# A drain on GpSimd's queue behind an expert's last gather, and row scatters without waits for one another

## The chip, the cores and the metric

One core of one Trainium2 chip runs the kernel in one launch. The metric is the device time of that launch in microseconds, as the median of several runs. The engines are named as in the profile: PE (TensorE), DVE (VectorE), ACT (ScalarE), POOL (GpSimd), SP (SyncE); PEld is TensorE's weight loading. A name with a q behind it (POOLq) means the instructions of that engine's queue: waits, branches, drains.

## What is computed

Attention with two kinds of masks, a dense feed-forward layer, and a layer of eight experts of which each token visits one, on 2304 tokens of width 512. The last of the three is what the change is in:

```python
def _moe2_ref(x, w_skip, w_gate, w1, w2):
    do_compute = x @ w_skip > 0
    out = x.copy()
    xc = x[do_compute]
    logits = xc @ w_gate
    e_idx = np.argmax(logits, axis=1)
    probs = softmax(logits)
    gate_w = probs[np.arange(len(xc)), e_idx]
    for e in range(E):
        mask = e_idx == e
        h = np.maximum(xc[mask] @ w1[e], 0.0)
        y[mask] = gate_w[mask, None] * (h @ w2[e])
    out[do_compute] = xc + y
```

## The kernel before

Attention and the dense layer run first, in an order that a planner in the kernel writes out. The routing is done block by block beside them: `route_list` (L822, 18 DMAs issued by GpSimd) writes each token's number and weight into the list of its expert, `lst`. The layer's result goes into `out` and `x2d` in DRAM, so a token that visits no expert is done.

`experts()` then goes through the lists in tiles of 128 tokens, four tiles to a group. `gather` (L888) reads four tiles of rows out of `x2d` by four indirect DMAs of GpSimd; `turn` transposes them; `up` (L920) is the first matrix of the expert, `down` (L933) the second, one output tile of 128 rows after the other. For each such tile VectorE scales the result and adds the gathered row (`row`, L937), and GpSimd scatters the tile into `out` (L938), an indirect DMA that writes each row where the list says. The places come from the list alone; entries behind a list's end are outside the bounds and write nothing.

Which expert comes first is guessed before the routing ends, and its weights and first four tiles are fetched early. The rest of a list is worked off by `groups`: full groups of four tiles under nested conditions, and then `rest` with the one to three tiles left over. The group's gather for what comes next is issued inside the group that comes before it. So `rest` gathers four tiles for the next expert (L1093) between the first two and the last six of its eight steps of `up`, and then its own `down` scatters its tiles.

With these inputs one expert has the list: one early group of four tiles (its scatters stand under L1057 and L1076 in the program's conditions), three full groups, and `rest` with two tiles (the branch of L1106). The loop over further experts (L1117, L1118) is not entered. Behind the loop the program ends (L1376): each engine drains, SyncE waits for the semaphores' last values, and the engines meet in an exchange of semaphores that GpSimd leads.

The framework sets the waits. GpSimd's DMAs count their landings on eight semaphores, the lanes DMASW0 to DMASW7, used in turn. Two writes into the same DRAM tensor are put in order: a scatter into `out` waits until the scatter before it has landed. Where a branch is not taken, an instruction of GpSimd (INC_SWDGE_SEM, "ISA" in the order) raises the lanes by what the branch would have added: all eight at the end of L1076, one in the branch of L1106, all eight at L1117. VectorE writes rows into three buffers in turn, and waits for the scatter that last read the buffer.

Of the kernel before, what the change touches and what calls it, by code (L numbers as in the profile page):

```python
# [189 lines left out]
def kernel(  # L190
# [18 lines left out]
    PE, V, A, G, SY = nc.tensor, nc.vector, nc.scalar, nc.gpsimd, nc.sync  # L209
# [542 lines left out]
    def route_a(blk):  # L752
        d = rt[blk]
        lg = d["lg"]
        l8 = lg[:, :, 0:8]
        mx = sp.tile([128, 12], F32, name="mx")
        e8 = sp.tile([128, 3, 8], F32, name="e8")
        d.update(mx=mx, e8=e8)
        V.tensor_reduce(mx[:, 0:3], l8, axis=AX.X, op=ALU.max)
        V.tensor_tensor(e8[:], l8, bc(mx[:, 0:3]), op=ALU.is_equal)  # L760
        V.tensor_tensor(l8, l8, bc(mx[:, 0:3]), op=ALU.subtract)
# [4 lines left out]
    def route_exp(blk):  # L766
        d = rt[blk]
        d["x8"] = sp.tile([128, 3, 8], F32, name="x8")
        A.activation(d["x8"][:], d["lg"][:, :, 0:8], AF.Exp)
# [21 lines left out]
    def route_c(blk):  # L791
        d = rt[blk]
        mx = d["mx"]
        d["pay"] = pay = sp.tile([128, 3, 2], I32, name="pay")
        V.tensor_reduce(mx[:, 9:12], d["x8"][:], axis=AX.X, op=ALU.add)
        V.tensor_scalar_add(mx[:, 9:12], mx[:, 9:12], 1e-9)
        V.reciprocal(pay[:, :, 1].bitcast(F32), mx[:, 9:12])
        V.tensor_copy(pay[:, :, 0], toks[:, 3 * blk:3 * blk + 3])
# [31 lines left out]
    def reg(t, c, hi, on=None):  # L830
        kw = {} if on is None else {"engines": on}
        return nc.values_load(t[0:1, c], min_val=0, max_val=hi, skip_runtime_bounds_check_because=WHY, **kw)

    def tally(cn):
        PE.matmul(cn[:, 0:8], one, cum[0][:, 3, :], start=True, stop=True)
# [48 lines left out]
    def gather(gi, n=NT):  # L884
        gx = sp.tile([128, 4], I32, name="gx")
        V.tensor_copy(gx[:], gi)
        for t in range(4):
            G.indirect_dma_start(  # L888
                K["R"][t], None, x2d[0:n, :], bass.IndirectOffsetOnAxis(ap=gx[:, t:t + 1], axis=0),
                bounds_check=n - 1, oob_is_err=False,  # L890
            )
# [22 lines left out]
    def up(N, f0=0, f1=NFE):  # L914
        for f in range(f0, f1):
            p = ph.tile([128, 512], F32, name="h")
            n = 0
            for w, x in ((0, K["Xh"]), (1, K["Xh"]), (0, K["Xl"])):
                for k in range(4):
                    PE.matmul(p[:, 0:N], W[f][:, w, k * 128:(k + 1) * 128], x[:, k, 0:N], start=n == 0, stop=n == 11)  # L920
                    n += 1
            h = K["h"][f]
            A.activation(h[:, 0, 0:N], p[:, 0:N], AF.Relu)  # L923
            V.scalar_tensor_tensor(h[:, 1, 0:N], p[:, 0:N], 0.0, h[:, 0, 0:N].bitcast(F32), op0=ALU.max, op1=ALU.subtract)  # L924

    def down(nt, ids, rows, t0=0):
        for t in range(t0, nt):
            c = slice(t * 128, (t + 1) * 128)
            y = px.tile([128, DM], F32, name=f"x2p{K['ny'] % 3}")
            n = 0  # L930
            for f in range(NFE):
                for g, w in ((0, 0), (1, 0), (0, 1)):
                    PE.matmul(y[:], K["h"][f][:, g, c], W[NFE + f][:, w, :], start=n == 0, stop=n == 3 * NFE - 1)  # L933
                    n += 1
            yo = rp.tile([128, DM], F32, name="row")
            K["ny"] += 1
            V.scalar_tensor_tensor(yo[:], y[:], ids[:, t, 1:2].bitcast(F32), rows[t], op0=ALU.mult, op1=ALU.add)  # L937
            G.indirect_dma_start(  # L938
                out, bass.IndirectOffsetOnAxis(ap=ids[:, t, 0:1], axis=0),
                yo[:], None, bounds_check=NT - 1, oob_is_err=False,  # L940
            )

# [73 lines left out]
    def keep_rows():  # L1018
        for t in range(4):
            A.copy(K["E"][:, t, :], K["R"][t])  # L1020

    def experts():
        K["h"] = [wp.tile([128, 2, 512], F32R, name=f"wo{8 + f}") for f in range(NFE)]
        K["E"] = wp.tile([128, 4, DM], F32, name="xb2")
        E = [K["E"][:, t, :] for t in range(4)]
        npre = reg(pre, slice(3, 4), NT)

        def fill(n):
            lo, hi = FILL[n], FILL[n + 1]
            if hi > lo:  # L1030
                with tc.If(npre >= 512):
                    up(512, lo, hi)

        last_x2(fill)
        route_a(NBLK - 1)
        route_exp(NBLK - 1)
        route_b(NBLK - 1)
        route_c(NBLK - 1)
        keep_rows()
        fill(3)  # L1040
        rk, cn = (pm.tile([128, 512], F32, name=n_) for n_ in ("sx0", "sx1"))
        route_rank(NBLK - 1, rk)
        tally(cn)
        route_out(NBLK - 1)
        route_list(rt[NBLK - 1])
        lt = sp.tile([128, NL, 2], I32, name="s_")
        gi = sp.tile([128, NL], I32, name="pts", bufs=1)
        SY.dma_start(lt[:, 0:NE * NTT, :].rearrange("p (e t) c -> p e t c", e=NE), lst[:].rearrange("(e p t) c -> p e t c", p=128, t=NTT))
        fill(4)
        finish_routing(cn)  # L1050
        V.memset(gi[:], NT - 1)
        V.tensor_scalar(gi[:, 0:NE * NTT], lt[:, 0:NE * NTT, 0], NT - 1, None, op0=ALU.min)
        on = (mybir.EngineType.DVE,)
        eg = reg(meta, slice(0, 1), NE - 1, on)
        s0 = reg(meta, slice(19, 20), 4, on)
        gather(gi[:, bass.ds(eg * NTT + s0, 4)])
        with tc.If(npre >= 512):  # L1057
            down(3, K["ltp"], E)
        def copied(e, t0, n):
            ids = sp.tile([128, 4, 2], I32, name="ids")  # L1060
            V.tensor_copy(ids[:, 0:n, :], lt[:, bass.ds(t0, n), :])
            return ids

        def group(e, g):
            ids = copied(e, e * NTT + 4 * g, 4)
            up(512, 0, 2)
            keep_rows()
            gather(gi[:, bass.ds(e * NTT + 4 * g + 4, 4)])
            up(512, 2)
            turn()  # L1070
            down(4, ids, E)

        word = reg(meta, slice(28, 29), (NE << 16) + 0xFFFF)
        e0, e1, T, ni = word & 7, (word >> 3) & 7, (word >> 6) & 31, word >> 16
        turn()
        with tc.If(npre >= 512) as done:  # L1076
            down(4, K["ltp"], E, 3)
        with done.Else():
            for n in range(8):
                load_raw(e0, n)  # L1080
            for n in range(2 * NFE):
                split_w(n)
            with tc.If(T >= 4):
                group(e0, 0)
        for n in range(8):
            load_raw(e1, n)

        def rest(e, T, en, r):
            if r:
                ids = copied(e, e * NTT + (T & 28), r)  # L1090
                up(max(256, 128 * r), 0, 2)
                keep_rows()
            gather(gi[:, bass.ds(en * NTT, 4)])  # L1093
            if r:
                up(max(256, 128 * r), 2)
                down(r, ids, E)

        def groups(e, T, en):
            with tc.If(T >= 8):
                group(e, 1)  # L1100
                with tc.If(T >= 12):
                    group(e, 2)
                    with tc.If(T >= 16):
                        group(e, 3)
            with tc.If((T & 2) == 2) as two:
                with tc.If((T & 1) == 1) as one_more:  # L1106
                    rest(e, T, en, 3)
                with one_more.Else():
                    rest(e, T, en, 2)
            with two.Else():  # L1110
                with tc.If((T & 1) == 1) as one_more:
                    rest(e, T, en, 1)
                with one_more.Else():
                    rest(e, T, en, 0)

        groups(e0, T, e1)
        with tc.If(ni > 1):  # L1117
            with tc.For_i(1, ni, 1) as i:  # L1118
                turn()
                word = reg(meta, bass.ds(i + 20, 1), 0x7FF)  # L1120
                e, en, T = word & 7, (word >> 3) & 7, word >> 6
                for n in range(2 * NFE):
                    split_w(n)
                for n in range(8):
                    load_raw(en, n)
                with tc.If(T >= 4):
                    group(e, 0)
                groups(e, T, en)
# [251 lines left out]
```

## Time and profile before

| what | value |
|---|---|
| median of 3 runs | 748.25 us (748.14 to 749.53) |
| the profiled execution's own time | 752.28 us |
| its span, first to last instruction | 750.5 us |
| TensorE busy | 726.4 us, 97% of the span |
| GpSimd busy | 62.9 us, 8%, 67 instructions |
| mean granted TensorE clock | 0.987 |
| GpSimd's DMA queue (q0) | 3936 packets, 11.03 MB |

Busy time counts an engine's own work; waits, branches, drains and semaphore increments of a queue are not in it, and are found by asking for the source line they belong to. For an indirect DMA of GpSimd the busy time is that of the instruction; when the data has landed is told apart, as the time from issue to landing.

### The profile page before, as it was taken

How to read it: one execution, taken by the hardware profiler on the slowest of the kernel's cores; microseconds unless marked ns; L12 is line 12 of the kernel's file. 1: busy time of each engine (PE TensorE's matmuls, PEld its weight loads, DVE VectorE, ACT ScalarE, POOL GpSimd, SP SyncE). 2: the span in 40 equal slices, each digit the busy share in tenths (PEclk: the TensorE clock that was granted, in tenths of full speed). 3: DMA queues.
4: the chain of work that ended last, by engine and by line, in shares of the span. 5: the costliest groups of instructions: out<-in, count | busy, mean ns of one | idle time of the engine just before them, and what ended most of it. 6: DMA issues, size and time to landing. Idle time of an engine off the chain costs nothing.

```text
span 750.5 us, 12212 instructions
## 1 busy us (share of the span) xinstructions
PE 726.4 (97%) x4516; PEld 624.6 (83%) x4517; DVE 399.8 (53%) x1092; ACT 294.2 (39%) x819; POOL 62.9 (8%) x67
## 2 busy tenths in 40 slices
PE   8899999999999999999999999999999999999992
PEld 6788788998888888888889898898787888888891
DVE  4889899935554744788546655644432312213120
ACT  3867776524353554544432224433301402113020
POOL 0000000000010100000100012110032212012121
PEclk9989999999999999999999999999999999999997
DMA  9775656302230222432031105310114512011131
GB/s 296 257 236 173 202 174 185 105 1 85 90 137 13 73 81 72 139 105 57 18 99 43 43 15 185 127 55 16 69 47 146 212 42 71 15 43 56 44 72 32
DMA packets 26895, 73.74 MB, mean 98 GB/s; under 512 B 5557, under 2 KB 5813, under 8 KB 26821
## 3 DMA queue, kind: packets, MB, share of 16 engines
q1 hardware_dynamic: 22741, 61.56, 25.4%
q0 software_dynamic: 3936, 11.03, 4.5%
q8 instruction: 41, 0.67, 0.4%
q14 instruction: 33, 0.27, 0.1%
q10 hardware_dynamic: 144, 0.22, 0.1%
HBM read 57.67 MB, written 15.13 MB: 97 GB/s over the span
## 4 chain that ended last, share of the span: by engine, by line
PE 86%; DVE 5%; issue 3%; ACT 3%; DMA 1%; POOL 0%; POOLq 0%; SPq 0%; DVEq 0%; ACTq 0%
PE h L1147 25%; PE x2p L1190 24%; PE h L920 12%; PE x2p L933 11%; PE sx L455 2%; PE pt L433 2%; PE sx L399 2%; PE sx L401 1%; PE h L1300 1%; DMA out<-row,ids 1%; DMA wo<-in_w_out 1%; DVE xb L462 1%; PE x2p L983 1%; PE sx L666 1%; PE pt L652 1%
## 5 line engine op out<-in xcount | busy, mean ns | idle before, releaser
L1147 PE MATMUL h<-xb,wi 128*128 128x384 f32 x1152 | 223.4, 343 | 1.2 <-ACT r L1152 1.2
L1147 PEld LDWEIGHTS h<-xb,wi 128*128 128x128 f32 x1152 | 204.0, 189 | 8.5 <-ACT r L1152 1.6
L1190 PE MATMUL x2p<-wo,gh 128*128 128x512 f32 x564 | 195.3, 400 | 0.0
L1190 PEld LDWEIGHTS x2p<-wo,gh 128*128 128x128 f32 x564 | 106.5, 189 | 21.2
L1190 PE MATMUL x2p<-wo,gl 128*128 128x512 f32 x282 | 111.2, 395 | 0.0
L920 PE MATMUL h<-xb,wi 128*128 128x512 f32 (+1 forms) x480 | 103.3, 374 | 1.4 <-DVE row L937 1.0
L920 PEld LDWEIGHTS h<-xb,wi 128*128 128x128 f32 x480 | 83.5, 188 | 19.3 <-issue 1.6
L933 PE MATMUL x2p<-wi,wo 128*128 128x512 f32 x432 | 99.4, 390 | 0.0
L1152 ACT ACTIVATE r<-h 128x384 f32<-128x384 f32 x96 | 47.0, 490 | 128.7 <-PE h L1147 113.0
L933 PEld LDWEIGHTS x2p<-wi,wo 128*128 128x128 f32 x432 | 80.7, 188 | 16.6
L1155 DVE SCALAR_TENSOR_TENSOR r<-r,sbc 128x384 f32<-128x384 f32 x88 | 54.2, 616 | 75.2 <-ACT r L1152 74.9
L923 ACT ACTIVATE wo<-h 128x512 fp32r<-128x512 f32 (+1 forms) x40 | 22.2, 555 | 142.1 <-PE h L920 137.2
L1159 ACT ACTIVATE gh<-r,sbc 128x384 fp32r<-128x384 f32 x88 | 54.3, 617 | 53.5 <-DVE r L1155 30.3
L1164 DVE SCALAR_TENSOR_TENSOR gl<-r,sbc,gh 128x384 fp32r<-128x384 f32 x88 | 54.2, 616 | 33.2 <-ACT gh L1159 27.4
L924 DVE SCALAR_TENSOR_TENSOR wo<-h,wo 128x512 fp32r<-128x512 f32 (+1 forms) x40 | 25.5, 638 | 75.4 <-ACT wo L923 75.4
L822 POOL DMA_INDIRECT lst<-pay,ii x18 | 18.4, 1023 | 500.7 <-DVE ii L816 274.0
L1190 PEld LDWEIGHTS x2p<-wo,gl 128*128 128x128 f32 x282 | 53.3, 189 | 8.1
L937 DVE SCALAR_TENSOR_TENSOR row<-x2p,ids,xb 128x512 f32<-128x512 f32 x14 | 10.5, 751 | 61.8 <-PE x2p L933 61.8
L703 DVE SCALAR_TENSOR_TENSOR junk<-row,lo 128x512 int8<-128x512 f32 x54 | 37.2, 689 | 7.5 <-DMA lo<-wgt 6.6
L462 DVE TENSOR_TENSOR xb<-sx,xb 128x192 fp32r<-128x192 f32 (+4 forms) x64 | 19.6, 333 | 9.9 <-ACT xb L277 7.2
L277 ACT CAST xb<-sx 128x192 fp32r<-128x192 f32 (+4 forms) x56 | 15.9, 337 | 19.5 <-PE sx L401 8.1
L938 POOL DMA_INDIRECT out<-row,ids x14 | 13.9, 995 | 107.5 <-DVE row L937 93.2
(481 smaller groups left out, 771.1 us busy)
## 6 DMA issues: line engine op xcount, KB each, us to landing
wo<-in_w SPq DMA_DIRECT2D x16, 512.0 KB
wo<-in_w_out SPq DMA_DIRECT2D x12, 512.0 KB
x2d<-row SPq DMA_DIRECT2D x21, 256.0 KB
qks<-in_qkstr SPq DMA_DIRECT2D x6, 882.0 KB
wo<-in_w_in SPq DMA_DIRECT2D x10, 512.0 KB
out<-row SPq DMA_DIRECT2D x18, 256.0 KB
lo<-wgt SPq DMA_DIRECT2D x18, 256.0 KB
qkl<-in_qkloc SPq DMA_DIRECT2D x5, 864.0 KB
```

The costliest lines, as they stand in the source:

```text
L462: V.tensor_tensor(dst(1), src(d["xo"]), dst(0).bitcast(F32), op=ALU.subtract)
L703: V.scalar_tensor_tensor(junk[:], d["rows"][t][:], 1.0, wd["w"][:], op0=ALU.mult, op1=ALU.mult, accum_out=d["lg"][:, t, x:x + 1])
L920: PE.matmul(p[:, 0:N], W[f][:, w, k * 128:(k + 1) * 128], x[:, k, 0:N], start=n == 0, stop=n == 11)
L923: A.activation(h[:, 0, 0:N], p[:, 0:N], AF.Relu)
L924: V.scalar_tensor_tensor(h[:, 1, 0:N], p[:, 0:N], 0.0, h[:, 0, 0:N].bitcast(F32), op0=ALU.max, op1=ALU.subtract)
L933: PE.matmul(y[:], K["h"][f][:, g, c], W[NFE + f][:, w, :], start=n == 0, stop=n == 3 * NFE - 1)
L1147: PE.matmul(p[:, 0:BLK], win_t[fc][:, w, k * 128:(k + 1) * 128], x[:, k, :], start=n == 0, stop=n == 11)
L1152: A.activation(d["r"][:], d["p"][:, 0:BLK], AF.Relu)
L1155: V.scalar_tensor_tensor(d["r"][:], d["r"][:], sbc[:, 0:1], d["r"][:], op0=ALU.mult, op1=ALU.mult)
L1159: A.activation(gh[:], d["r"][:], AF.Identity, bias=sbc[:, 1:2])
L1164: V.scalar_tensor_tensor(gl[:], d["r"][:], sbc[:, 1:2], gt[i][0][:].bitcast(F32), op0=ALU.add, op1=ALU.subtract)
L1190: PE.matmul(x2p[t][:], g[:, c], wout_t[fc][:, w, :], start=begins and n == 0, stop=ends and n == 2)
```

## The change

Two edits. A scatter into `out` is declared independent of the other scatters into `out` (they form a group "rows" whose members are not put in order among themselves). And in `rest` a drain stands on GpSimd's queue behind the gather.

```diff
@@ down
-            G.indirect_dma_start(
+            put = G.indirect_dma_start(
                 out, bass.IndirectOffsetOnAxis(ap=ids[:, t, 0:1], axis=0),
                 yo[:], None, bounds_check=NT - 1, oob_is_err=False,
             )
+            tc.declare_no_dep(put.ins, group="rows", reason="the lists name each token once")
+            tc.add_to_no_dep_group("rows", put.ins)
@@ rest
             gather(gi[:, bass.ds(en * NTT, 4)])
+            G.drain()
             if r:
```

The order of the other engines' instructions is the same. On GpSimd's queue, in `rest` with two tiles (L1106), the four gathers and the two scatters stood so, with the semaphores that each waits for (DVE, PE, Activation: those engines' counts):

```order
L888 DMA qkl<-x2d,gx 128x512 [waits DMASW5_49,DVE_49,DMASW6_49,PE_49,Activation_49]
L888 DMA qkl<-x2d,gx 128x512 [waits DMASW7_49,PE_49,Activation_49]
L888 DMA qks<-x2d,gx 128x512 [waits DMASW0_49,PE_49,Activation_49]
L888 DMA qks<-x2d,gx 128x512 [waits DMASW1_49,PE_49,Activation_49]
L938 DMA out<-row,ids 2304x512 [waits DMASW4_49,DMASW3_49,DMASW5_49,DMASW2_49,DVE_49]
L938 DMA out<-row,ids 2304x512 [waits DMASW2_49,DVE_49]
L1106 ISA [waits DMASW4_49]
```

And now, at the same place of the changed program (its lines behind the first edit are two or three higher):

```order
L888 DMA qkl<-x2d,gx 128x512 [waits DMASW5_49,DVE_49,DMASW6_49,PE_49,Activation_49]
L888 DMA qkl<-x2d,gx 128x512 [waits DMASW7_49,PE_49,Activation_49]
L888 DMA qks<-x2d,gx 128x512 [waits DMASW0_49,PE_49,Activation_49]
L888 DMA qks<-x2d,gx 128x512 [waits DMASW1_49,PE_49,Activation_49]
L938 DMA out<-row,ids 2304x512 [waits DMASW2_49,DVE_49]
L938 DMA out<-row,ids 2304x512 [waits DMASW3_49,DVE_49]
L1109 ISA [waits DMASW4_49]
```

The first of the two scatters counts on lane 2 and the second on lane 3. Before, the second waited for lane 2, that is for the first; now each waits for its own lane's last use, in an earlier group, and for VectorE's row. The drain stands between the last gather and the first scatter; drains are not among the rows of the order.

## Rows read from the trace of the kernel before

**Rows 1.** The page's head: span; busy time of each engine.

```profile
span 750.5 us, 12212 instructions
PE 726.4 (97%) x4516; PEld 624.6 (83%) x4517; DVE 399.8 (53%) x1092; ACT 294.2 (39%) x819; POOL 62.9 (8%) x67
```

**Rows 2.** Chain that ended last, its end: start us, us, what.

```profile
732.04 5.59 DMA out<-row,ids
```

**Rows 3.** Timeline from 730 us: start, us, engine, line, op, tiles [idle before, releaser].

```profile
729.68 6.73 PE L933 MATMUL x2p<-wi,wo 128*128 128x512 f32 x29
...
731.02 0.75 DVE L937 SCALAR_TENSOR_TENSOR row<-x2p,ids,xb 128x512 f32<-128x512 f32 x1 [4.55 <-PE x2p L933]
732.04 1.03 POOL L938 DMA_INDIRECT out<-row,ids  x1 [8.92 <-DVE row L937]
736.46 0.75 DVE L937 SCALAR_TENSOR_TENSOR row<-x2p,ids,xb 128x512 f32<-128x512 f32 x1 [4.69 <-PE x2p L933]
738.44 1.00 POOL L938 DMA_INDIRECT out<-row,ids  x1 [5.37 <-DMA out<-row,ids]
```

**Rows 4.** Windows: stretch, its length, busy PE PEld DVE ACT POOL, PEclk, DMA share, GB/s.

```profile
744.70:750.50 5.80, 0.00 (x0) 0.00 (x0) 0.00 (x0) 0.00 (x0) 0.00 (x0) 0.50 0.00 0
```

**Rows 5.** Lines L1106 and L1117, POOL: ns min/median/max, first and last start.

```profile
L1106 POOLq INC_SWDGE_SEM  x1: 1355/1355/1355, 738.5 to 738.5; - x1
...
L1117 POOLq EVENT_SEMAPHORE  x6: 17/30/43, 742.8 to 743.2; - x6
...
L1117 POOLq COMPARE_BRANCH  x1: 50/50/50, 740.1 to 740.1; - x1
L1117 POOLq INC_SWDGE_SEM  x1: 1372/1372/1372, 743.3 to 743.3; - x1
```

**Rows 6.** Line L1376 (the program's end) on POOL's queue.

```profile
L1376 POOLq EVENT_SEMAPHORE  x4: 17/17/17, 749.7 to 750.4; - x4
L1376 POOLq DRAIN  x3: 46/103/4971, 744.7 to 750.2; - x3
```

**Rows 7.** Line L1376 on SP's queue, from 740 us.

```profile
L1376 SPq EVENT_SEMAPHORE  x14: 17/28/28, 744.6 to 750.5; - x14
L1376 SPq DRAIN  x3: 7/7/13, 745.4 to 749.9; - x3
```

**Rows 8.** Timeline of POOL: the last gather of the last branch.

```profile
722.13 0.99 POOL L888 DMA_INDIRECT qks<-x2d,gx  x1 [0.31 <-issue]
```

**Rows 9.** Line L1370 (the program's start) on POOL's queue.

```profile
L1370 POOLq INC_SWDGE_SEM  x1: 27/27/27, 0.2 to 0.2; - x1
...
L1370 POOLq DRAIN  x1: 188/188/188, 0.3 to 0.3; - x1
```

**Rows 10.** DMA issues of GpSimd: tiles, count, median us to landing.

```profile
lst<-pay,ii POOLq DMA_INDIRECT x18, 2.1
out<-row,ids POOLq DMA_INDIRECT x14, 2.8
...
qkl<-x2d,gx POOLq DMA_INDIRECT x12
qks<-x2d,gx POOLq DMA_INDIRECT x12, 4.0
out<-row,s__5047 POOLq DMA_INDIRECT x4, 3.0
```

**Rows 11.** Line L888, the gathers issued before 576 us.

```profile
L888 POOL DMA_INDIRECT qkl<-x2d,gx x4: 1012/1029/1043, 462.5 to 558.9; - x4
L888 POOL DMA_INDIRECT qks<-x2d,gx x4: 998/998/1456, 465.2 to 561.5; - x4
```

**Rows 12.** Line L938 from 738 us: landing of the second scatter.

```profile
DMA to landing us min/median/max: 3.5/3.5/3.5
```

**Rows 13.** Line L888, 721.9 to 724 us: landing of the last gather.

```profile
DMA to landing us min/median/max: 4.9/4.9/4.9
```

**Rows 14.** Line L1076 on POOL's queue: the increment at the early group's end.

```profile
L1076 POOLq INC_SWDGE_SEM  x1: 799/799/799, 575.5 to 575.5; - x1
```

## The prediction

> **What bounds the kernel now.** I read the page's head first, then the chain that ended last, then the timeline of the end, then the queues' own instructions at the end. The head says that TensorE works through 97% of the span [rows 1]: what happens beside it is hidden, and a change to GpSimd's queue can show only where TensorE has stopped. The chain ends in the wait of one scatter for the other: 5.59 us on the landing of the first scatter of the last branch, then the second [rows 2]. The timeline shows where TensorE stops: its last matmul ends at 736.4 us, and the row addition behind it runs from 736.46 to 737.21 [rows 3]. From there to 750.5 us are 13.3 us without a matmul. In this tail the change can show.
>
> The reader is to see the tail as one string of GpSimd instructions [rows 3, 5, 6]. The second scatter starts at 738.44. The semaphore increment behind it (INC_SWDGE_SEM of L1106) starts at 738.5 and takes 1.355 us, to 739.9. A branch at 740.1 is followed by 2.6 us without a row, until the waits of L1117 begin at 742.8. A second increment starts at 743.3 and takes 1.372 us, to 744.7. Then a DRAIN takes 4.971 us, to 749.7, and the closing exchange of semaphores ends the span 0.8 us later. SyncE's own closing waits start at 744.6 (they need the increment) and its drains stand at 745.4, 7 and 13 ns long [rows 7]. So only GpSimd's drain separates 745.5 from 749.7, and in 744.7 to 750.5 no DMA moves anything [rows 4].
>
> **The change part by part.** The changed kernel does three things to GpSimd's queue, and leaves the other engines' orders alone.
>
> (a) The second scatter no longer waits for the first. It needs only its row (737.21) and the landing of the DMA that last used its lane, one of an earlier branch. The scatter before it started 0.27 us after its row: 731.02 + 0.75 = 731.77, start 732.04 [rows 3]. So it starts at 737.48 in place of 738.44: **-0.96 us**. The same waits go in the other sixteen scatters [rows 10]: worth nothing, as TensorE is at work beside them until 736.4. What is late next is the landing. The second scatter landed 3.5 us after its start [rows 12]; from 737.48 that is 741.0. The worst row is the 5.59 us of the first [rows 2], which would be 743.1.
>
> (b) The added drain stands behind the fourth gather, whose issue ends at 722.13 + 0.99 = 723.12 [rows 8]. GpSimd's next work is the scatter at 732.04, so 8.9 us lie free there. Queued behind the drain are this branch's two scatters, nothing else; TensorE and VectorE wait for none of it before the last row. No row shows a drain in the middle of the program. The lower bound is the drain at the program's start, 0.188 us [rows 9]. The upper bound is one that begins to count its 4.971 us only when the last gather has landed: 722.13 + 4.9 [rows 13] = 727.0, plus 5.0 = 732.0. Both end before or at the first scatter's start, so it costs **0**. If the cover were gone, each microsecond past it would shift the first scatter, and past some 5 us more the second.
>
> (c) What the last drain then costs. It is not waiting for data: all DMAs had landed by 741.9 (738.44 + 3.5), 2.8 us before it began. It is not a price of every drain: the two behind it take at most 103 ns, the first of the program 188 ns [rows 6, 9]. The difference between these is what came before: 60 DMAs that GpSimd issued (18 + 14 + 12 + 12 + 4) [rows 10] against none. If it works through each DMA issued since the last drain, that is 4971 / 60 = 83 ns each. With a drain behind the 58th, two are left: 0.17 us and the 0.188 of an empty one, some 0.4 us. SyncE is then the last to arrive, at 745.5 in today's times; the end moves by 749.7 - 745.5 = **-4.2 us**. The bounds: nothing, if each drain has a fixed price, and 4.2 us, beyond which SyncE holds the end.
>
> The Trainium skill (VectorE: DVE Perf Modes, section The DRAIN you can't avoid) says that the drains of preamble and postamble are a constant of about 12 ns on all five engines. By that figure there would be nothing to move, and the sum would be (a) alone; SyncE's 7 and 13 ns agree with it [rows 7], GpSimd's 4,971 ns [rows 6] does not.
>
> (d) The increments. The one at 575.5 took 0.799 us, when 30 DMAs had been issued (18 + 8 + 4) [rows 10, 11, 14]; the two at the end took 1.355 and 1.372 us, after 60. The first raised all eight lanes and the second only one, so the number of lanes does not explain it; the number of DMAs does, if what the drain clears is what an increment looks through. Bounds: no change, or down to 0.2 us (the straight line through 30 and 60 DMAs gives 18.5 ns each, and 0.24 us at none). I take 0.80 for both, the row with the fewest DMAs, and no lower since it stood beside a scatter, as one of the two will: 0.55 + 0.57 = **-1.1 us**.
>
> Sum: -0.96 - 4.2 - 1.1 = -6.3 us. In this order GpSimd reaches its wait for the second landing (it stood shortly before 743.3) at about 741.7, after the 741.0 of the landing, so that bound is not yet reached. The profiled execution has a span of 750.5 us and its own time was 752.28 us, so it would read 746.0; it stands 4.0 us above the median of the shown runs, 748.25 us. I take the gain off the median: **742.0 us**. With (d) at nothing it is 743.1; with (d) at its full bound, 2.2 us, it is 740.9; with the second scatter landing as late as the first, some 1.5 us is given back, 743.5.
>
> **The rivals.** A measurement of this kernel tells a change of about 0.2%, 1.5 us, from none.
>
> Rival 1: a drain that follows any DMA has a fixed price, such as one look at each of 16 DMA engines (311 ns each would fill the 4.971 us). Then the added drain pays it unseen at 723, the last one pays it again for two scatters, and the increments stay as they are. For it: one long row cannot tell a count from a constant. Against it: nothing had been outstanding for 2.8 us when the drain began, and the empty ones are short. Only (a) is left: 748.25 - 0.96 = **747.3 us**. The skill's rule above is of this kind, a constant price, with another figure. That the drain does not do what it says (that it only stops the queue, and clears nothing) gives the same time and is counted here.
>
> Rival 2, on the other side: the added drain holds GpSimd longer than its cover. Its place has what the last one had not, four gathers in flight, the last of which lands 4.9 us after its issue [rows 13]. It decides from the point where the second scatter comes later than today: back-to-back DMAs are 1.30 us apart (0.31 + 0.99) [rows 8], so the drain must end after about 738.44 - 1.30 - 0.27 = 736.9, 13.8 us after it began, 2.8 times the longest drain seen. From there each microsecond is one at the end. If it took 18 us and the last drain were not shortened, the time would be 748.25 + 4.2 = **752.5 us**. Against it: the upper bound above, 732.0.
>
> **How the numbers follow.** The forecast, a price by count that the earlier drain takes over, with the increments and the landing anywhere within their bounds: 0.76. Rival 1: 0.19. Rival 2: 0.05. The predicted time is the forecast's, 742.0. Its own range is 740.9 to 743.5. That holds too little of the chance, so the range goes on to rival 1 and reads 740.5 to 747.5, with 0.4 us at the low end and 0.2 at the high for the spread of the runs. Faster by over 0.2% (under 746.75) is the forecast alone, 0.76; within 0.2% is rival 1, 0.19; slower is rival 2, 0.05.
>
> **What would show it.** In the profile of the changed kernel: a DRAIN on GpSimd's queue at about 723 us of some 4.5 to 5 us; the second scatter 0.3 us behind the last row addition; the two increments shorter than 1.3 us; the closing drain under 0.5 us; SyncE's closing waits ending last; a span of about 744. A closing drain still near 5 us would be rival 1, and the forecast wrong in (c). Increments still at 1.36 us would make (d) wrong, and cost 1.1 us. A first scatter that starts later than 732.1 would tell that the cover of (b) is thinner than I count.

## The result, and the profile after

The changed kernel took **741.89 us** (median of 6 runs, 741.30 to 744.54), the kernel before 749.38 us on the same chip (6 runs, 748.14 to 751.49). The ratio is 0.991, with a 95% interval of 0.989 to 0.993: by the ratio 6.8 us less (5.1 to 8.5 by the interval), by the medians 7.5. The forecast was 742.0 us. The profiled execution of the changed kernel took 741.30 us itself, with a span of 739.5 us.

The page's head, to be held against [rows 1], shows the same work on every engine (the matmuls' counts differ by records that are missing, and TensorE's 3.1 us less goes with a mean granted clock of 0.992 in place of 0.987):

```profile
span 739.5 us, 12203 instructions
PE 723.3 (98%) x4513; PEld 623.0 (84%) x4517; DVE 400.1 (54%) x1092; ACT 294.1 (40%) x819; POOL 62.7 (8%) x67
```

The two profiled spans differ by 11.0 us, more than the medians. The last matmul ends at 736.4 us before and 732.5 after; from there to the end of the span are 14.1 and 7.0 us. Only this tail belongs to the change. Executions of one kernel differ by up to 4.7 us (747.13 to 751.79 for the kernel before, over 17 runs), and the two traces lie 4.1 us apart from the first list write on, ahead of every scatter and of the added drain. Line L822 before and after (first and last start):

```profile
L822 POOL DMA_INDIRECT lst<-pay,ii x18: 969/970/1336, 205.0 to 550.9; - x18
L822 POOL DMA_INDIRECT lst<-pay,ii x18: 967/970/1332, 200.9 to 546.5; - x18
```

The medians agree: the median less the tail of the profiled execution is 735.3 us for before, 734.8 for after, and 734.5 to 734.9 for the five later kernels that only leave out, move or repeat parts of the change. So what follows compares tails, each from the one trace of its kernel.

The timeline of the end (start, us, engine, line, operation, tiles [idle before, releaser]), against [rows 3]:

```profile
724.82 7.64 PE L933 MATMUL x2p<-wi,wo 128*128 128x512 f32 x33
...
727.06 0.75 DVE L937 SCALAR_TENSOR_TENSOR row<-x2p,ids,xb 128x512 f32<-128x512 f32 x1 [4.55 <-PE x2p L933]
728.09 1.03 POOL L938 DMA_INDIRECT out<-row,ids  x1 [8.90 <-DVE row L937]
732.50 0.75 DVE L937 SCALAR_TENSOR_TENSOR row<-x2p,ids,xb 128x512 f32<-128x512 f32 x1 [4.69 <-PE x2p L933]
733.53 1.00 POOL L938 DMA_INDIRECT out<-row,ids  x1 [4.42 <-DMA out<-row,ids]
```

The last row is ready at 732.50 + 0.75 = 733.25 and its scatter starts at 733.53, 0.28 us later; before it was 1.23 us. The releaser in the brackets still reads "DMA out", though the scatter no longer waits for the one before it: it waits for an earlier landing on its lane, long past, and for the row. The gap of 0.28 us, that of the first scatter too, shows that the row came last.

The queue's own instructions on POOL: the added drain, the increment of the last branch, the stretch behind the loop, and the program's end (count: ns min/median/max, first and last start), against [rows 5, 6]:

```profile
L1096 POOLq DRAIN  x1: 9552/9552/9552, 715.8 to 715.8; - x1
...
L1109 POOLq INC_SWDGE_SEM  x1: 203/203/203, 733.3 to 733.3; - x1
...
L1120 POOLq EVENT_SEMAPHORE  x6: 17/30/43, 737.2 to 737.6; - x6
...
L1120 POOLq COMPARE_BRANCH  x1: 55/55/55, 734.0 to 734.0; - x1
L1120 POOLq INC_SWDGE_SEM  x1: 226/226/226, 737.7 to 737.7; - x1
...
L1379 POOLq EVENT_SEMAPHORE  x4: 17/17/17, 738.7 to 739.4; - x4
L1379 POOLq DRAIN  x3: 46/103/212, 738.0 to 739.3; - x3
```

And the program's end on SP's queue, against [rows 7]:

```profile
L1379 SPq EVENT_SEMAPHORE  x14: 17/28/28, 737.9 to 739.5; - x14
L1379 SPq DRAIN  x3: 7/7/13, 738.6 to 739.0; - x3
```

The closing drain fell from 4,971 to 212 ns and ends at 738.2. SyncE's first drain starts at 738.6, and the exchange that ends the program begins behind it: SyncE is the last to arrive, as forecast. The increments fell from 1,355 and 1,372 ns to 203 and 226. Step by step, with the tail of before beside it:

| step of the tail | before, us | after, us | difference |
|---|---|---|---|
| row ready to start of second scatter | 1.23 | 0.28 | -0.95 |
| row ready to end of first increment (holds the step above) | 2.69 | 0.24 | -2.44 |
| first increment's end to end of the branch | 0.30 | 0.61 | +0.31 |
| branch to the first wait behind it, nothing shown | 2.58 | 3.07 | +0.49 |
| second increment | 1.372 | 0.226 | -1.15 |
| second increment's end to the exchange (drain before, SyncE after) | 5.0 | 0.8 | -4.25 |
| last matmul to end of the span | 14.11 | 7.08 | -7.03 |

The second step is 0.34 us shorter than the two shorter parts in it, the scatter's start and the increment, make it: before, the increment starts 0.10 us behind the scatter's row; now it starts 0.24 us ahead of it, at 733.29.

### The profile page after: what moved, and what is told of

It is laid out like the page before. It is cut to its first block, busy times and chain, and to the rows that moved or that the text cites. A ratio compares the mean times of both kernels' runs of the same rounds, so it can differ in the third digit from the quotient of the medians.

```text
span 739.5 us, 12203 instructions
## 1 busy us (share of the span) xinstructions
PE 723.3 (98%) x4513; PEld 623.0 (84%) x4517; DVE 400.1 (54%) x1092; ACT 294.1 (40%) x819; POOL 62.7 (8%) x67
## 3 DMA queue, kind: packets, MB, share of 16 engines
q0 software_dynamic: 3936, 11.03, 4.7%
## 4 chain that ended last, share of the span: by engine, by line
PE 81%; issue 5%; DVE 5%; DMA 4%; ACT 3%; POOL 1%; SPq 0%; POOLq 0%; ACTq 0%; DVEq 0%
PE h L1150 25%; PE x2p L1193 24%; PE h L920 10%; PE x2p L933 8%; DMA out<-row,ids 4%; PE sx L455 2%; PE pt L433 2%; PE sx L399 2%; PE sx L401 1%; PE h L1303 1%; DVE xb L462 1%; DMA wo<-in_w_out 1%; PE x2p L985 1%; PE sx L666 1%; PE pt L652 1%
## 5 line engine op out<-in xcount | busy, mean ns | idle before, releaser
L822 POOL DMA_INDIRECT lst<-pay,ii x18 | 18.4, 1022 | 496.3 <-DVE ii L816 474.5
L938 POOL DMA_INDIRECT out<-row,ids x14 | 14.0, 997 | 106.1 <-DVE row L937 92.7
```

## The experiments

Two theories stood against each other. The forecast's: a drain works through each DMA that GpSimd has issued since the drain before, and an increment looks through the same list, so the added drain takes the work over, unseen. Its rival: a drain has a fixed price, or the gain came from the scatters' order. Six kernels ran. Where the sketch of an edit says "the changed kernel", the rest is as in the change.

**One part alone: without the drain.**

```diff
@@ rest (the changed kernel)
             gather(gi[:, bass.ds(en * NTT, 4)])
-            G.drain()
```

> The scatters without waits, and no added drain. Count theory (the closing drain pays some 83 ns for each GpSimd DMA since the last drain, the increments some 20 ns): the second scatter starts 0.3 us behind the last row addition instead of 1.2, the closing drain stays at 4.9 to 5.0 us and the increments at 1.35 us, the tail behind the last matmul (14.1 us before, 7.0 us with both edits) is about 13.1 us, the time 0.96 us under before: 0.1%, which cannot be told from no change by the times. Rival (the waits between scatters are the cause, and the drain only comes earlier because of them): the closing drain falls under 1 us and the tail to 8 us or less.

Measured: 748.51 us (12 runs, 747.27 to 750.76), ratio 0.998 (0.997 to 1.000). On POOL, the timeline and the queue's rows:

```profile
736.13 1.00 POOL L938 DMA_INDIRECT out<-row,ids  x1 [4.42 <-DVE row L937]
```

```profile
L1108 POOLq INC_SWDGE_SEM  x1: 1356/1356/1356, 735.9 to 735.9; - x1
...
L1119 POOLq EVENT_SEMAPHORE  x6: 17/30/43, 740.9 to 741.3; - x6
...
L1119 POOLq COMPARE_BRANCH  x1: 50/50/50, 737.8 to 737.8; - x1
L1119 POOLq INC_SWDGE_SEM  x1: 1372/1372/1372, 741.4 to 741.4; - x1
```

```profile
L1378 POOLq DRAIN  x3: 46/103/4971, 742.8 to 748.4; - x3
```

The row was ready at 735.85, so the scatter follows by 0.28 us: the wait is gone. The increments and the closing drain are those of before to the nanosecond or two. The tail is 13.58 us against 14.11 before, where 13.1 was expected. So the scatters' order shortens neither increment nor drain; of the 0.95 us some 0.5 reaches the end, since the stretch from the branch to the next wait now takes 3.1 us (737.8 to 740.9) in place of 2.6.

**The other part alone: the drain, and the scatters in order.**

```diff
@@ down (the changed kernel)
-            tc.declare_no_dep(put.ins, group="rows", reason="the lists name each token once")
-            tc.add_to_no_dep_group("rows", put.ins)
```

> The added drain alone; the scatters wait for one another as before. Count theory: the closing drain is 0.2 us and the increments 0.2 us as with both edits, the second scatter starts about 1.0 us later than it does there, and the tail is about 8.0 us (7.0 + 1.0); the time is some 6.1 to 6.5 us under before, 1 us over the kernel with both edits. Rival (the waits are needed for the gain): a tail of 12 us or more.

Measured: 742.30 us (6 runs, 741.91 to 744.10), ratio 0.990 (0.988 to 0.992), not to be told from the whole change, though 1 us more was expected. Its rows on POOL's queue:

```profile
L1107 POOLq INC_SWDGE_SEM  x1: 202/202/202, 734.2 to 734.2; - x1
```

```profile
L1377 POOLq DRAIN  x3: 46/103/213, 738.6 to 739.9; - x3
```

The tail is 7.74 us, 0.66 more than with both parts. The drain brings all but about 0.7 us of the gain. What holds GpSimd here is the landing. The waits behind the loop, on POOL's queue:

```profile
L1118 POOLq EVENT_SEMAPHORE  x6: 17/30/422, 737.4 to 738.2; - x6
```

One of the six takes 422 ns, where the longest of the changed kernel takes 43. The second scatter in POOL's timeline, and its landing by line L938 from 733 us:

```profile
734.38 1.00 POOL L938 DMA_INDIRECT out<-row,ids  x1 [5.31 <-DMA out<-row,ids]
```

```profile
DMA to landing us min/median/max: 3.7/3.7/3.7
```

So it landed at 738.1, and this wait ends just behind it.

**A count in between: the drain earlier.** It stands behind the last list write, 22 DMAs into the program; 38 follow it.

```diff
@@ experts (the changed kernel, its drain in rest left out)
         route_list(rt[NBLK - 1])
+        G.drain()
```

> Scatters without waits; the one added drain stands earlier, behind the last three list writes, so that 22 of the 60 DMAs lie before it and 38 behind it. Count theory: the early drain takes about 1.8 us beside its wait for landings, the closing drain about 38 x 83 ns = 3.2 us, the two increments at the end about 0.9 us each, that of the early group about 0.3 us; the tail is about 11 us, the time 3 us under before. Rival (the first drain behind DMAs costs about 5 us once, whatever their number, and later ones little): the closing drain is 0.2 us and the tail about 7.0 us, as with the drain in the last branch. Rival (the time hangs on the time since the last DMAs, not on their number): closing drain near 5 us.

Measured: 746.06 us (4 runs, 745.36 to 748.70), ratio 0.994 (0.992 to 0.996). The early drain, the three increments and the program's end on POOL's queue:

```profile
L1048 POOLq DRAIN  x1: 3299/3299/3299, 549.6 to 549.6; - x1
```

```profile
L1079 POOLq INC_SWDGE_SEM  x1: 363/363/363, 574.5 to 574.5; - x1
```

```profile
L1109 POOLq INC_SWDGE_SEM  x1: 916/916/916, 736.2 to 736.2; - x1
```

```profile
L1120 POOLq INC_SWDGE_SEM  x1: 932/932/932, 742.0 to 742.0; - x1
```

```profile
L1379 POOLq DRAIN  x3: 46/103/3167, 742.9 to 746.7; - x3
```

The closing drain takes 3,167 ns for 38 DMAs, 83 ns each, where it took 4,971 for 60. A fixed price is out: the drain is neither 5 us nor near nothing, but in proportion. The increment that took 0.799 us after 30 DMAs [rows 14] takes 0.363 with 8 since the drain. The tail is 11.55 us, where about 11 was expected.

**More DMAs, no drain added.** The kernel before, with each list write made three times with the same values: 96 DMAs in place of 60. It tells a price by count from one by bytes, for the 36 added ones are small.

```diff
@@ route_list (the kernel before)
-        for t in range(3):
+        for t in [0, 1, 2] * 3:
```

> The kernel before, in which each list write of the routing is issued three times, the second and third with the same values: 54 small list writes of GpSimd instead of 18, so 96 DMAs instead of 60, with 36 KB more data. Count theory: the closing drain takes 96 x 83 ns = 7.9 us instead of 4.97, the increments at the end about 2.1 us instead of 1.36, that of the early group about 1.5 us instead of 0.80; the tail grows by about 4.4 us, to 18.5. Rival (a fixed or one-time price): closing drain 4.97 us, tail 14.1. Rival (a price by bytes): the same as fixed, since the added writes are small. The wait for the last lists also grows by the added issues, up to some 5 us in the middle of the program; that part is read apart, by the time of the last matmul.

Measured: 776.11 us (4 runs, 773.44 to 776.61), ratio 1.033 (1.031 to 1.036). The end, the increments and the queue's total:

```profile
L1376 POOLq DRAIN  x3: 46/103/7911, 765.6 to 774.1; - x3
```

```profile
L1076 POOLq INC_SWDGE_SEM  x1: 1503/1503/1503, 595.3 to 595.3; - x1
```

```profile
L1117 POOLq INC_SWDGE_SEM  x1: 2092/2092/2092, 763.5 to 763.5; - x1
```

```profile
q0 software_dynamic: 5088, 11.07, 4.5%
```

The 36 added writes carry 0.04 MB in 1,152 packets, 32 each, where the other 42 DMAs carry 80 packets each (3,936 - 18 x 32, by 42). They lengthen the closing drain by 7,911 - 4,971 = 2,940 ns, 82 ns each. The 38 behind the early drain, gathers and scatters alone, took 83 each. So the price goes by the number of DMAs, not by packets or bytes. Each of all these DMAs has 128 indices, so that a price by index cannot be told here from one by DMA. The tail is 18.39 us, as expected. The body was missed: its last matmul ends 19.5 us later than before (some 22.5 by the medians less the tails), where at most some 5 were expected. Line L822 of this kernel (the writes of the lists, and what POOL's idle time before them ended in: us, times) shows why:

```profile
L822 POOL DMA_INDIRECT lst<-pay,ii x54: 969/969/1361, 203.4 to 571.5; - x54
...
  DMA lst<-pay,ii: 84.5, 48
```

Each list write waits until the one before has landed. These waits come to 84.5 us where the kernel before has 22.9, and the last write starts at 571.5 where it started at 550.9: the experts' gathers, behind it on the queue, are 20.6 us late.

**Less for the added drain to do: a drain behind every group's gather.** The added drain of `rest` then has 8 DMAs to go through (the last group's four scatters, and its own four gathers) in place of 58. It tests what the drain's length is made of.

```diff
@@ group (the changed kernel)
             gather(gi[:, bass.ds(e * NTT + 4 * g + 4, 4)])
+            G.drain()
```

> Both edits, and a drain behind the gather of each full group too, so that the drain of the last branch has 8 DMAs to look through (four scatters, four gathers) instead of 58. Count theory: closing drain 0.21 us and increments 0.2 us as with one drain, tail about 7.1 us, the time that of the changed kernel within 0.2%; the drain of the last branch, 9.55 us with 58 DMAs, ends some 0.7 us behind the landing of its last gather and takes about 7.7 us. Rival (its length is the wait for the gathers and a settled time behind it, not the number): it ends about 2.4 us behind the last landing again and takes 9.5 us.

Measured: 741.91 us (4 runs, 741.53 to 742.91), ratio 0.989 (0.987 to 0.992). The drains of the groups, and that of `rest`:

```profile
L1071 POOLq DRAIN  x3: 6516/7035/9612, 582.4 to 674.3; - x3
```

```profile
L1097 POOLq DRAIN  x1: 7622/7622/7622, 717.1 to 717.1; - x1
```

The drain of `rest` still shows 7.6 us, though only 8 DMAs stand before it. Its row starts before the third and fourth gather are issued (718.19 and 719.50 in the timeline of this kernel), so the row's length holds the issue and the flight of the gathers. The last gather landed at 724.39 by its semaphore's event, and the drain ends at 724.76, 0.37 us behind, where some 0.7 was expected. In the changed kernel, with 58 DMAs, the last gather landed at 722.96 and the drain ends at 725.38, 2.42 us behind. Behind the landing only a part of the price is left, and it too goes by count. The tail is 7.29 us: neither kernel's drain reaches the end.

**Nothing of its own in flight: the drain ahead of the last gather.**

```diff
@@ rest (the changed kernel)
+            G.drain()
             gather(gi[:, bass.ds(en * NTT, 4)])
-            G.drain()
```

> Both edits, the drain put ahead of the last branch's four gathers instead of behind them: no gather in flight, 54 DMAs to look through, 6 left for the closing drain. Count theory: the drain takes about 54 x 82 ns = 4.4 us and the rest of the scatter issued just before it, some 5 to 5.5 us; the four gathers start about 1.5 to 2 us later; closing drain 0.05 + 6 x 0.082 = 0.54 us, increments 0.28 us; SyncE still arrives last, tail 7.1 to 7.3 us, the time that of the changed kernel within 0.2%. Rival (the drain's length was a wait for the gathers): under 2 us here.

Measured: 742.21 us (4 runs, 741.49 to 744.69), ratio 0.990 (0.987 to 0.994). The drain, the first gather behind it in POOL's timeline, and the end:

```profile
L1095 POOLq DRAIN  x1: 4917/4917/4917, 711.9 to 711.9; - x1
```

```profile
717.82 1.04 POOL L888 DMA_INDIRECT qkl<-x2d,gx  x1 [5.48 <-DVE wo L924]
```

```profile
L1379 POOLq DRAIN  x3: 46/103/539, 739.4 to 740.7; - x3
```

Now six DMAs are left, and the closing drain takes 539 ns, as expected. The drain itself takes 4.92 us, where 5 to 5.5 was expected and under 2 by the rival. It holds the gathers back: counted from the start of the scatter before them, the first starts 6.45 us later (711.37 to 717.82), in the changed kernel 3.81 (710.40 to 714.21). That is 2.6 us more, where 1.5 to 2 was expected. No further expert follows in this run and nothing waits for these gathers, so the tail, 7.57 us, tells nothing of what that delay may cost. It is 0.3 us above what was expected, and the stretch behind the branch is 0.35 us longer here than in the changed kernel (3.41 and 3.06).

All closing drains on one line, 0.048 us and 82 ns for each DMA since the last drain:

| DMAs since the last drain | 2 | 6 | 38 | 60 | 96 |
|---|---|---|---|---|---|
| closing drain, us | 0.212 | 0.539 | 3.167 | 4.971 | 7.911 |
| the line, us | 0.212 | 0.540 | 3.16 | 4.97 | 7.92 |
| last increment, us | 0.226 | 0.293 | 0.932 | 1.372 | 2.092 |

The Trainium skill (VectorE: DVE Perf Modes, section The DRAIN you can't avoid) says that the runtime's boilerplate drains, those of the preamble and postamble, are a constant of about 12 ns on all five engines. SyncE's rows, 7 to 13 ns, agree with it; GpSimd's closing drain, 0.21 to 7.9 us, does not.

## Why the prediction was right, and where a term was off

The time, 742.0 us forecast and 741.89 measured, came out right, and so did the mechanism that carried it. That the two lie 0.1 us apart is luck in part. The forecast took 6.3 us off 748.25 us; the kernel before had a median of 749.38 us beside the changed one, and 7.5 us less was measured (7.0 in the tail). The gain was forecast too small by about as much as the base was low.

**(a) The second scatter.** The start moved by 0.95 us, as forecast (0.96). Of it 0.5 to 0.7 us reaches the end (tails of 14.11 and 13.58 without the drain, 7.74 and 7.08 with it). The sum took all of it; the unshown stretch behind the branch grew, and with the drain the landing lies close. The landing, named as late next, was close: the second scatter started at 733.53, its landing by line L938 of the changed kernel, from 727 us, is

```profile
DMA to landing us min/median/max: 3.8/3.8/3.8
```

behind the start, 737.3, and GpSimd's wait for it stands at 737.45. With some 0.2 us more it would have held GpSimd up, as it did where the scatters kept their order. The scatter's own row ends 2.8 us before that. The Trainium skill (Perfetto Trace Analysis, section DMA Instruction — SWDGE (GPSIMD)) says that the profiler ends such a row when the descriptors have been written, not when the data has arrived; this row and this landing agree.

**(b) The added drain.** It costs nothing, as forecast. It ends at 725.38. The queue's rows of the two scatters, line L938 from 725 us on, show what follows:

```profile
L938 POOLq MOVE  x2: 29/29/29, 725.4 to 727.8; - x2
L938 POOLq EVENT_SEMAPHORE  x2: 17/17/17, 725.5 to 727.9; - x2
```

The first move and the first wait, for lane 2, belong to the first scatter and are done at 725.51; it then waits for its row, ready at 727.06 + 0.75 = 727.81. So 2.3 us of cover are left. Its row was foreseen at about 723 us with 4.5 to 5 us, in the times of before; it shows 9.55 us, since it begins while gathers are still to be issued. Counted from the end of the fourth gather's issue, 718.19 + 1.00, it takes 6.2 us, between the bounds of 0.2 and 8.9. The upper bound assumed that the whole price begins at the last landing; it was 2.42 us in place of 5.

**(c) The closing drain.** Forecast some 0.4 us and an end 4.2 us earlier, with SyncE last; measured 0.212 us, 4.25 us, and SyncE last. The price by count, drawn from one long row and a count of 60, is shown by four further counts.

**(d) The increments.** Here the size was off. Each was taken at 0.80 us, the row after 30 DMAs, and 1.1 us were counted; they take 0.203 and 0.226, which is 2.3 us less, the full bound (down to 0.2 us each is 2.3 us, not the 2.2 of the sum). The straight line through 30 and 60 DMAs, named there (18.5 ns each, 0.24 us at none), was the better guide: the runs give about 20 ns each and 0.16 to 0.21 us at none, and before, the one beside a scatter took 1.355 us, the one alone 1.372. What was added for caution was the error.

This added 1.2 us to the gain, and the first increment's start ahead of the scatter's row another 0.34. Of these, 0.8 was given back between the first increment and the waits of L1120 (the two rows with a plus in the table), which no term of the sum held.

**The rivals.** Rival 1, a fixed price, forecast 747.3 us. It falls with the drain placed early, and the run without the drain, 748.5 us, shows what is left when the drain clears nothing. Rival 2, a drain that outlasts its cover, did not come; the cover left over is 2.3 us. A second expert was not tried.

## What to carry to other kernels

The drain on GpSimd at this program's end has a price that grows with the DMAs that the queue has issued since the drain before, 82 ns for each; if that drain ends last, put one where GpSimd is idle, behind as many of the DMAs as fit and ahead of the last ones. The conditional branches' increments become cheaper with it (1.36 to 0.20 us here). Look for such instructions by their source line, for the busy times of the page hold none of them, and count what stands before them: one long row together with a count gave the price here, and kernels with other counts showed that it is one.

## What the runs showed that was not expected

- A drain that begins while DMAs are in flight has about half of its price left behind the last landing. It ended 0.37 us behind it with 8 DMAs to go through (three drains of the kernel with a drain in every group), 0.95 with 22 (the early drain), 1.44 with 34 (that kernel's first group) and 2.42 with 58 (the changed kernel): 0.05 us and 41 ns for each, where the closing drain takes 82. The drain ahead of the last gathers, with 54, ended 2.55 us behind the landing of the scatter before it, where that line gives 2.26; but from the end of that scatter's row, 712.35, it took 4.49 us, and the full price of 54 is 4.48. All of these fit a drain that has half of its price from the last issue on, and the other half behind the last landing. That it works so is argued, not shown. The landings are those of the semaphores' events.
- The increment's time goes by the same count, at about 20 ns for each DMA, and the number of lanes that it raises adds little: 203 ns for one lane and 226 for eight, in the changed kernel. Even these 23 ns need not be the lanes', for the first of the two ends before the second scatter's row begins.
- From GpSimd's branch out of the loop over experts to its first wait behind it, 2.6 us pass in the kernel before (740.1 to 742.8) and 3.1 in the changed one (734.0 to 737.2), with no row on its queue; in the eight profiles it is 2.6 to 3.7 us. It is now the largest piece of the 7.1 us of tail. In each of the eight, packets of queue q14, which the page lists as instruction, are moved within the stretch (in the kernel before at 740.3 and 741.1 us, 8 KB each). So the loading of instructions is a candidate; that GpSimd waits for it is not shown. Cause and spread stay open; no run tried them.
